# A two-layer H3 and MLP kernel: sums, powers and stage order of the normalisation between its first two units

## The chip, the cores and the metric

The kernel runs on one core of one Trainium2 chip. The metric is the device time in microseconds (us) of one execution. A core has five engines that run side by side, each in the order of its own instructions: TensorE (PE) multiplies matrices, VectorE (DVE), ScalarE (ACT) and GpSimd (POOL) work on elements, and SyncE (SP) starts transfers here. Semaphores order the engines among each other. On chip there are SBUF (128 partitions) and PSUM, where matrix products arrive.

## The reference

Two kinds of layer alternate, A, B, A, B, each added to its input. With S = 2048 tokens, D = 1024 channels and F = 3584 hidden columns, all in float32:

```python
def _A_ref(q, k, v, shift_k, ssm_k, ssm_D):     # q is the normalised x
    k_shift = short causal convolution of k with shift_k (4 taps)
    kv = k_shift * v
    y  = long causal convolution of kv with ssm_k (length S, by FFT) + kv * ssm_D
    return q * y

def _B_ref(x, w1, b1, w2, b2):                  # x is normalised
    h = relu(x @ w1 + b1) ** 2
    return h @ w2 + b2

x = A_q
x = x + _A_ref(_layernorm(x), ...);  x = x + _B_ref(_layernorm(x), ...)
x = x + _A_ref(_layernorm(x), ...);  x = x + _B_ref(_layernorm(x), ...)
```

The inputs k and v of the convolution do not depend on x, so the long convolution y is computed once and used by both A layers. The normalisation subtracts the row's mean and divides by the root of its variance plus 1e-5.

## The kernel before

Tokens are worked in four blocks of 512 (four tiles of 128 rows each, numbered 0 to 3 within the block). A unit is the B layer of one block at one depth, and ORDER lists them: layer 0 of block 0, layer 1 of block 0, layer 0 of block 1, layer 0 of block 2, and so on. Only the first change of units stays with its block (`direct`): unit 1 needs what unit 0 just finished. It therefore has to gate and normalise between two matrix products, while the other units are prepared beforehand.

A unit is a list of steps. A step of kind m1 multiplies one weight tile of w1 (128x512) with the transposed activations; one of kind m2 multiplies the squared activations with a tile of w2. Every product is done as three matmuls on numbers split into a high and a low part: the weight is loaded (`w_load`), its high part is cast on ScalarE (`w_hi`, L1112), the low part is a subtraction on VectorE or GpSimd (`w_lo`, L1120, engine by the table WLO); some split weights are stored and come back as pairs by one transfer (L1108). `w_advance` (L1130) issues all this some three steps ahead of the use, as far as six buffers go.

Around the first change of units the steps are halved, so that one half of the block (tiles 0 and 1) can be gated and normalised while TensorE works on the other: `add_halves` (L934) makes 28 m2 half steps, first both output halves for tiles 0 and 1, then for tiles 2 and 3; `add_ahead` (L950) makes 24 m1 half steps for six hidden tiles of unit 1, twelve for tiles 0 and 1, twelve for tiles 2 and 3. In half steps `tts` names two tiles, and so `len(tts) < NT`.

The work between is done by `chain` (L1737). When the accumulators of a half are complete, `evict1` adds the products to the residual (L1778) and takes statistics (L1779), and `lag.at(d, stage, cst, kk)` puts the stages 0 to 10 on a list, each d steps later; `lag.tick()` runs, once a step, what is due. The numbers d are the two rows of CHAIN. Stage 0 aggregates the statistics and starts a root on ScalarE (L732), stage 1 makes the scale by eight small VectorE operations (L738 to L754 and L1754). Stage 2 gates both tiles: ScalarE normalises a half row into PSUM (L1760), VectorE multiplies with y (L1767), adds to x (L1769) and takes statistics again (L1773). Stages 3 and 4 repeat the scale, 5 and 6 normalise the two tiles (L1808 on ScalarE, L1810 on VectorE, by NORM), 7 and 8 transpose them on TensorE (L1819), 9 and 10 split them into xh and xl (L1827, L1828). The tiles y come by `load_y` (L1731) into a ring of two buffers.

Beside the units, two generators prepare the long convolution of later blocks. The forward streams (`fwd_x`, `fwd_g`, one `fwd_tick` for both) transform kv and the filter; the product stream (`prod_stream`) multiplies spectra on GpSimd (L546) and sums them on VectorE (L550). At the end of each step the products get a budget: `pace` per step, a tenth of it in half steps; where the product stream has to wait for a transform (it yields None), the forward streams get a tick more. In half steps that is the only tick they get, since the line below (L2321) gives none. At the first half step of the change `closed[0] = True` (L2266) keeps the streams from taking the two PSUM banks "pt", and a loop runs the streams on until both are free.

The order inside a step is written in the main loop (L2163): in half steps of kind m1 (phase "x") the weights come first and the list after; in all others the list comes first.

Of the kernel before, what the change touches and what calls it, by code (L numbers as in the profile page):

```python
# [10 lines left out]
F32 = mybir.dt.float32  # L11
F32R = mybir.dt.float32r
BF16 = mybir.dt.bfloat16
AF = mybir.ActivationFunctionType
OP = mybir.AluOpType
# [4 lines left out]
S, D, F = 2048, 1024, 3584  # L20
P = 128
T = 512
NT = T // P
# [30 lines left out]
PLAIN = 1  # L54
PAD_C, PAD_P, PAD_M = 104, 104, 32
FILL = (16, 0, 8)
# [11 lines left out]
KEEP_M = 4  # L68
CHAIN = ((2, 3, 3, 7, 8, 8, 9, 13, 13, 14, 14), (2, 3, 3, 7, 8, 8, 9, 12, 12, 13, 13))
NORM = "VAVA"  # L70
WLO = {"b": "G", "x": "GGGV", "e": "G", "b1": "VVG", "c2": "VVG"}
# [180 lines left out]
def tile_h3_mlp(ctx: ExitStack, tc: tile.TileContext, q, kT, vT, shk, ssmT, ssmD, w1, b1, w2, b2,  # L252
# [474 lines left out]
    def rstd_a(mv):  # L727
        n = mv.shape[1]
        ve = pre.tile([P, n], F32, name="ve", bufs=3)
        V.tensor_scalar(ve, mv[:, :, 1], EPS, None, op0=OP.add)  # L730
        sd = pre.tile([P, n], F32, name="sd", bufs=3)
        A.activation(sd, mv[:, :, 1], AF.Sqrt, bias=epst)  # L732
        return ve, sd
# [1003 lines left out]
    def chain(accs, b, xh, xl, ready):  # L1737
        def bn(st, h):
            for n, tt in enumerate(st["tts"]):
                V.bn_stats(st["st"][:, n, h], accs[tt][:, h * 512:(h + 1) * 512])  # L1740

        def agg(st):
            mv = st["mv"] = pre.tile([P, 2, 2], F32, name="mv3", bufs=2)
            for n in range(2):
                V.bn_aggr(mv[:, n], st["st"][:, n])
            st["ve"], st["sd"] = rstd_a(mv)

        def newst(st):
            st["st"] = pre.tile([P, 2, 2, 6], F32, name="st3", bufs=2)

        def scales(st):
            r = st["r"] = rstd_b(st["ve"], st["sd"])
            st["nm"] = pre.tile([P, 2], F32, name="nm", bufs=3)
            V.scalar_tensor_tensor(st["nm"], st["mv"][:, :, 0], -1.0, r, op0=OP.mult, op1=OP.mult)  # L1754

        def scaled(st, n):
            out = []
            for h in range(2):
                z = ps1()
                A.activation(z, accs[st["tts"][n]][:, h * 512:(h + 1) * 512], AF.Identity,  # L1760
                             bias=st["nm"][:, n:n + 1], scale=st["r"][:, n:n + 1])
                out.append((h, z, accs[st["tts"][n]][:, h * 512:(h + 1) * 512], st["y"][n][:, h * 512:(h + 1) * 512]))
            return out

        def gate(ops):
            for h, z, x, y in ops:
                V.tensor_mul(z, z, y)  # L1767
            for h, z, x, y in ops:
                V.tensor_add(x, x, z)  # L1769

        def spread_of(st, n, ops):
            for h, z, x, y in ops:
                V.bn_stats(st["st"][:, n, h], x)  # L1773

        def evict1(st, os, dh):
            d = slice(dh * 512, (dh + 1) * 512)
            for n, tt in enumerate(st["tts"]):
                V.tensor_add(accs[tt][:, d], os[tt], accs[tt][:, d])  # L1778
                V.bn_stats(st["st"][:, n, dh], accs[tt][:, d])  # L1779

        def stage(st, k):
            tts = st["tts"]
            if k == 0:
                agg(st)
            elif k == 1:
                scales(st)
                newst(st)
            elif k == 2:
                ops = scaled(st, 0)
                gate(ops)  # L1790
                more = scaled(st, 1)
                spread_of(st, 0, ops)
                gate(more)
                spread_of(st, 1, more)
            elif k == 3:
                agg(st)
            elif k == 4:
                scales(st)
            elif k in (5, 6):
                n = k - 5  # L1800
                x, m, r = accs[tts[n]], st["mv"][:, n, 0:1], st["r"][:, n:n + 1]
                st["o", n] = []
                st["z", n] = [row() for _ in range(2)]
                for kh in range(2):
                    xn = st["z", n][kh]["t"]
                    xs = x[:, kh * 512:(kh + 1) * 512]
                    if NORM[2 * n + kh] == "A":
                        A.activation(xn, xs, AF.Identity, bias=st["nm"][:, n:n + 1], scale=r)  # L1808
                    else:
                        V.tensor_scalar(xn, xs, m, r, op0=OP.subtract, op1=OP.mult)  # L1810
                    st["o", n].append(xn)
            elif k in (7, 8):
# [8 lines left out]
                drop(*st["z", n])  # L1821
            else:
                n = k - 9
# [339 lines left out]
    for s, (k, u, c, a, i, tts, w) in enumerate(steps):  # L2163
# [30 lines left out]
        top = max(top, w)  # L2194
        if phase[0] == "x":
            w_advance(s, top)
            lag.tick()
        else:
            lag.tick()
            w_advance(s, top)  # L2200
# [105 lines left out]
        rate = pace.get(u, 100) * (PREP_PACE if busy else 1.0)  # L2306
        if len(tts) < NT:
            rate *= 0.1
        owed += rate
        todo = min(owed, BURST * rate)  # L2310
        while todo > 0:
# [63 lines left out]
```

## Time and profile before

| what | value |
|---|---|
| median of 3 runs | 2676.86 us (2676.43 to 2679.94) |
| the profiled execution, by the device clock | 2678.26 us |
| its span, first to last instruction | 2676.5 us |
| granted TensorE clock, mean | 0.995 |
| moved by transfers | 763.16 MB, mean 285 GB/s |
| splits of weights on VectorE (L1120, from raw weights) | 486 of 888 ns, 426.2 us |
| products on GpSimd (L546) | 288 of 1897 ns, 542.6 us |
| transposes of the chain (L1819) | 32, from 497.1 to 526.4 us |

The profile is of one execution, and its durations belong to that execution's 2678.26 us. "Busy" counts an engine from the start to the end of its instructions. Matmuls overlap, so TensorE's busy share says little of how fast it goes; the distance from one start to the next does. A row of waits names the engine and line that waited, the one that released it, the total, the number of waits and the longest. In rows of the timeline the first number is the start, the second the duration, and a bracket at the end gives idle time before it and what ended it. The granted clock is a share of full speed.

### The profile page before, as it was taken

How to read it: one execution, taken by the hardware profiler on the slowest of the kernel's cores; microseconds unless marked ns; L12 is line 12 of the kernel's file. 1: busy time of each engine (PE TensorE's matmuls, PEld its weight loads, DVE VectorE, ACT ScalarE, POOL GpSimd, SP SyncE). 2: the span in 40 equal slices, each digit the busy share in tenths (PEclk: the TensorE clock that was granted, in tenths of full speed). 3: DMA queues.
4: the chain of work that ended last, by engine and by line, in shares of the span. 5: the costliest groups of instructions: out<-in, count | busy, mean ns of one | idle time of the engine just before them, and what ended most of it. 6: DMA issues, size and time to landing. Idle time of an engine off the chain costs nothing.

```text
span 2676.5 us, 36110 instructions
## 1 busy us (share of the span) xinstructions
PE 2623.3 (98%) x12388; PEld 2198.9 (82%) x12388; DVE 1980.9 (74%) x2848; ACT 1133.8 (42%) x1931; POOL 1034.8 (39%) x683
## 2 busy tenths in 40 slices
PE   8899999899999999999999999999999999999999
PEld 7888787788888888888888888888788778888887
DVE  7878888789987777779777775456778767777553
ACT  5454344444444333343333422345444585454442
POOL 2436665255542645427554175000100217536111
PEclk9999999999999999999999999999999999999999
DMA  8799898689989998788987888689889798878653
GB/s 255 250 316 310 295 302 282 234 290 369 353 296 312 317 333 298 276 299 305 339 303 253 300 295 305 207 264 315 300 295 307 264 338 254 264 252 312 231 195 121
DMA packets 380265, 763.16 MB, mean 285 GB/s; under 512 B 44064, under 2 KB 159408, under 8 KB 377008
## 3 DMA queue, kind: packets, MB, share of 16 engines
q1 hardware_dynamic: 380080, 760.85, 83.3%
q8 instruction: 98, 1.61, 0.2%
q14 instruction: 87, 0.71, 0.1%
HBM read 583.49 MB, written 177.21 MB: 284 GB/s over the span
## 4 chain that ended last, share of the span: by engine, by line
PE 80%; DMA 6%; DVE 4%; ACT 2%; issue 1%; POOL 1%; SPq 0%; DVEq 0%; POOLq 0%; ACTq 0%
PE p L356 24%; PE p L357 24%; PE p L358 24%; PE pt L358 2%; PE pt L356 2%; PE pt L357 2%; DMA whl<-wd_m 2%; DMA wr<-w 1%; DMA wd_m<-whl 1%; DVE whl L1120 1%; DMA yt<-yd 0%; PE pt L412 0%; PE pt L441 0%; DMA cx<-xd 0%; PE pt L616 0%
## 5 line engine op out<-in xcount | busy, mean ns | idle before, releaser
L546 POOL TENSOR_TENSOR cp<-cx,cg 128x384 f32<-128x384 f32 (+5 forms) x288 | 542.6, 1897 | 569.2 <-DVE sm L550 374.6
L356 PE MATMUL p<-xh,whl 128*128 128x512 f32 (+1 forms) x1504 | 577.0, 384 | 6.3 <-DMA whl<-wd_m 5.7
L358 PE MATMUL p<-xh,whl 128*128 128x512 f32 (+1 forms) x1504 | 572.9, 381 | 3.3 <-DVE whl L1120 2.8
L357 PE MATMUL p<-xl,whl 128*128 128x512 f32 (+1 forms) x1504 | 572.8, 381 | 0.4 <-DVE xl L1515 0.4
L1112 ACT CAST whl<-wr 128x512 fp32r<-128x512 f32 x546 | 332.4, 619 | 466.4 <-PE p L358 275.1
L1120 DVE TENSOR_TENSOR whl<-wr,whl 128x512 fp32r<-128x512 f32 x486 | 426.2, 888 | 131.0 <-ACT whl L1112 130.3
L356 PE MATMUL p<-whl,rh 128*128 128x512 f32 x1204 | 477.1, 396 | 4.9 <-DMA whl<-wd_m 4.3
L357 PE MATMUL p<-whl,rh 128*128 128x512 f32 x1204 | 472.1, 392 | 2.5 <-POOL whl L1120 1.4
L358 PE MATMUL p<-whl,rl 128*128 128x512 f32 x1204 | 471.5, 392 | 0.0
L356 PEld LDWEIGHTS p<-xh,whl 128*128 128x128 f32 x1504 | 283.4, 188 | 61.1 <-DMA whl<-wd_m 2.5
L358 PEld LDWEIGHTS p<-xh,whl 128*128 128x128 f32 x1504 | 283.3, 188 | 58.3 <-DVE whl L1120 3.0
L357 PEld LDWEIGHTS p<-xl,whl 128*128 128x128 f32 x1504 | 283.5, 188 | 52.7 <-DVE xl L1515 0.6
L1607 DVE TENSOR_TENSOR rl<-wr,rh 128x512 fp32r<-128x512 f32 x140 | 142.2, 1016 | 177.9 <-ACT rh L1604 177.7
L356 PEld LDWEIGHTS p<-whl,rh 128*128 128x128 f32 x1204 | 227.9, 189 | 53.4 <-DVE fg L1716 3.3
L1120 POOL TENSOR_TENSOR whl<-wr,whl 128x512 fp32r<-128x512 f32 x60 | 87.3, 1458 | 475.9 <-ACT whl L1112 447.7
L357 PEld LDWEIGHTS p<-whl,rh 128*128 128x128 f32 x1204 | 227.9, 189 | 50.2 <-DVE whl L1120 2.7
L358 PEld LDWEIGHTS p<-whl,rl 128*128 128x128 f32 x1204 | 227.6, 189 | 48.0
L550 DVE TENSOR_REDUCE sm<-cp 128x128 f32<-128x384 f32 (+5 forms) x288 | 249.4, 874 | 10.2 <-POOL cp L546 10.2
L1599 ACT ACTIVATE wr<-p,b1t 128x512 f32<-128x512 f32 x138 | 95.3, 690 | 367.2 <-PE p L358 366.2
L1727 DVE TENSOR_TENSOR acc<-p,acc 128x512 f32<-128x512 f32 x152 | 100.0, 686 | 81.0 <-PE p L358 80.9
L696 POOL TENSOR_TENSOR sm<-sm 128x512 f32<-128x512 f32 x48 | 68.7, 1431 | 134.0 <-DVE sm L550 128.5
L356 PE MATMUL p<-whl,tq 128*128 128x512 f32 x276 | 107.4, 389 | 0.0
(393 smaller groups left out, 4280.5 us busy)
## 6 DMA issues: line engine op xcount, KB each, us to landing
whl<-wd_m SPq DMA_DIRECT2D x318, 512.0 KB, 5.5
wr<-w SPq DMA_DIRECT2D x442, 256.0 KB, 5.7
wd_m<-whl SPq DMA_DIRECT2D x70, 512.0 KB, 6.0
wr<-td SPq DMA_DIRECT2D x112, 256.0 KB, 5.0
cx<-xd SPq DMA_DIRECT2D x48, 512.0 KB, 5.9
cg<-gd SPq DMA_DIRECT2D x48, 512.0 KB, 6.8
tq<-hd SPq DMA_DIRECT2D x24, 1024.0 KB, 7.3
gd<-fg SPq DMA_DIRECT2D x72, 256.0 KB, 5.9
```

The lines of the kernel that those rows point to most:

```text
L356: PE.matmul(o, lh, rh, start=start, stop=False)
L357: PE.matmul(o, lh, rl, start=False, stop=False)
L358: PE.matmul(o, ll, rh, start=False, stop=stop)
L546: G.tensor_mul(pr.rearrange("p c i -> p i c"), xt[:, 0:j + 1], gt[:, j::-1])
L550: V.tensor_reduce(sm[:, ty, jj], st["pr"], axis=AX.X, op=OP.add)
L696: E.tensor_add(s[:, 1:3], s[:, 1:3], s[:, 0:1].to_broadcast([P, 2, s.shape[2]]))
L1112: A.copy(t[:, 0], raws[n]["t"])
L1120: ENG[e[n % len(e)]].tensor_sub(t[:, 1], raws[n]["t"], t[:, 0].bitcast(F32))
L1599: A.activation(r, st["o"], AF.Relu, bias=b1t[:, st["f"]:st["f"] + 1])
L1607: V.tensor_sub(st["lo"], st["r"]["t"], st["hi"].bitcast(F32))
L1727: V.tensor_add(accs[tt][:, d], o, accs[tt][:, d])
```

## The change

All of it concerns half steps, so the first change of units and, by the last two hunks, the eight half steps near the start.

- Sums: for the first tile of each half, the additions to the accumulator (`summed`) become one VectorE operation that also writes its row sum; ScalarE then squares the row with the mean as bias and sums it (`spread_a`). The second tile keeps VectorE's statistics.
- Powers: the scale is one addition, one power and one multiplication on GpSimd (`scale_of`), in place of the root on ScalarE and eight small operations on VectorE.
- Staged gating: stage 1 gates the first tile, stage 2 the second, stage 3 takes the second tile's statistics. CHAIN gets new due times, NORM another engine for one half row.
- Weights split ahead: in all half steps `w_advance` comes before `lag.tick()`.
- Products: none in half steps; the budget of a tenth is still added to what is owed.
- PAD_P pads a pool by 16 words a partition more.

```diff
-PAD_C, PAD_P, PAD_M = 104, 104, 32
+PAD_C, PAD_P, PAD_M = 104, 120, 32
-CHAIN = ((2, 3, 3, 7, 8, 8, 9, 13, 13, 14, 14), (2, 3, 3, 7, 8, 8, 9, 12, 12, 13, 13))
-NORM = "VAVA"
+CHAIN = ((2, 3, 5, 8, 9, 8, 10, 13, 13, 14, 14), (2, 3, 5, 7, 7, 6, 9, 11, 12, 12, 13))
+NORM = "AAVA"
...
+        def summed(st, n, d, z):
+            x = accs[st["tts"][n]][:, d * 512:(d + 1) * 512]
+            V.scalar_tensor_tensor(x, z, 1.0, x, op0=OP.mult, op1=OP.add, accum_out=st["c"][:, 4 + d:5 + d])
+
+        def spread_a(st):
+            c = st["c"]
+            V.tensor_scalar(c[:, 0:1], c[:, 4:5], c[:, 5:6], -1.0 / (root * D), op0=OP.add, op1=OP.mult)
+            junk = ml.tile([P, D], BF16, name="yt", bufs=2)
+            A.activation(junk, accs[st["tts"][0]], AF.Square, scale=1.0 / root, bias=c[:, 0:1], accum_out=c[:, 1:2])
+            scale_of(st, 0, c[:, 1:2], c[:, 0:1], root)
...
+        def scale_of(st, n, var, m, k):
+            o = st["rn"][:, n]
+            G.tensor_add(var, var, epst)
+            G.tensor_tensor(o[:, 0:1], var, eph[:, 1:2], op=OP.pow)
+            G.tensor_scalar(o[:, 1:2], m, o[:, 0:1], k, op0=OP.mult, op1=OP.mult)
...
-        def gate(ops):
-            for h, z, x, y in ops:
+        def gate(st, n, ops):
+            x = accs[st["tts"][n]]
+            for z, y in ops:
                 V.tensor_mul(z, z, y)
-            for h, z, x, y in ops:
-                V.tensor_add(x, x, z)
+            for h, (z, y) in enumerate(ops):
+                if n:
+                    V.tensor_add(x[:, h * 512:(h + 1) * 512], x[:, h * 512:(h + 1) * 512], z)
+                else:
+                    summed(st, 0, h, z)
...
         def evict1(st, os, dh):
             d = slice(dh * 512, (dh + 1) * 512)
-            for n, tt in enumerate(st["tts"]):
-                V.tensor_add(accs[tt][:, d], os[tt], accs[tt][:, d])
-                V.bn_stats(st["st"][:, n, dh], accs[tt][:, d])
+            t0, t1 = st["tts"]
+            summed(st, 0, dh, os[t0])
+            if dh == (t0 > 0) ^ 1:
+                spread_a(st)
+            V.tensor_add(accs[t1][:, d], os[t1], accs[t1][:, d])
+            V.bn_stats(st["st"][:, 0, dh], accs[t1][:, d])
...
         def stage(st, k):
             tts = st["tts"]
             if k == 0:
-                agg(st)
+                spread_v(st)
+                scale_v(st)
             elif k == 1:
-                scales(st)
+                st["g"] = scaled(st, 0)
+                st["old"] = dict(st)
                 newst(st)
+                gate(st, 0, st["g"])
+                spread_a(st)
             elif k == 2:
-                ops = scaled(st, 0)
-                gate(ops)
-                more = scaled(st, 1)
-                spread_of(st, 0, ops)
-                gate(more)
-                spread_of(st, 1, more)
+                gate(st, 1, scaled(st["old"], 1))
             elif k == 3:
-                agg(st)
+                for h in range(2):
+                    V.bn_stats(st["st"][:, 0, h], accs[tts[1]][:, h * 512:(h + 1) * 512])
+                spread_v(st)
             elif k == 4:
-                scales(st)
+                scale_v(st)
             elif k in (5, 6):
...
+                normal(st, k - 5)
...
-        if phase[0] == "x":
+        if len(tts) < NT:
             w_advance(s, top)
             lag.tick()
         else:
...
-        if len(tts) < NT:
-            rate *= 0.1
-        owed += rate
-        todo = min(owed, BURST * rate)
+        owed += rate * (0.1 if len(tts) < NT else 1.0)
+        todo = 0.0 if len(tts) < NT else min(owed, BURST * rate)
         while todo > 0:
```

More of the change, by code (lines that the diff above doesn't have):

```diff
@@ L1737, in chain, with spread_v, scale_v @@
     def chain(accs, b, xh, xl, ready):
[L1738 to L1754 removed]
+        root = math.sqrt(D)
+        def summed(st, n, d, z):
[7 more added lines that the diff above has]
+            scale_of(st, 0, c[:, 1:2], c[:, 0:1], root)
+        def spread_v(st):
+            st["mv"] = pre.tile([P, 1, 2], F32, name="mv3", bufs=2)[:, 0]
+            V.bn_aggr(st["mv"], st["st"][:, 0])
+        def scale_v(st):
+            scale_of(st, 1, st["mv"][:, 1:2], st["mv"][:, 0:1], -1.0)
+        def scale_of(st, n, var, m, k):
[3 more added lines that the diff above has]
+            G.tensor_scalar(o[:, 1:2], m, o[:, 0:1], k, op0=OP.mult, op1=OP.mult)
+        def newst(st):
+            st["st"] = pre.tile([P, 1, 2, 6], F32, name="st3", bufs=2)
+            st["c"] = pre.tile([P, 6], F32, name="nr", bufs=4)
+            st["rn"] = pre.tile([P, 2, 2], F32, name="mv2", bufs=4)
         def scaled(st, n):
@@ L1821, in stage @@
                 drop(*st["z", n])
-            else:
+            elif k > 8:
                 n = k - 9
```

32 lines of the change are left out of this document (14 added, 18 removed).

## The prediction

> **What bounds the kernel now.** I read the page first (engine shares), then the stages (busy time and granted clock by window), then TensorE's waits in the stretch that the change touches, then the timelines of single engines there.
>
> ```profile
> span 2676.5 us, 36110 instructions
> PE 2623.3 (98%) x12388; PEld 2198.9 (82%) x12388; DVE 1980.9 (74%) x2848; ACT 1133.8 (42%) x1931; POOL 1034.8 (39%) x683
> ```
>
> TensorE is the bound: it idles 53.2 us in all, and only matmuls that start late can be won or lost. So the question is where those idle stretches lie, and the rows by window answer it (us, then busy time and count of PE, PEld, DVE, ACT, POOL, then granted clock, DMA share, GB/s).
>
> ```profile
> 250.00:300.00 50.00, 43.04 (x197) 35.68 (x195) 43.30 (x63) 19.36 (x36) 28.95 (x24) 0.96 0.90 305
> 300.00:350.00 50.00, 49.80 (x225) 41.88 (x226) 36.88 (x59) 18.91 (x35) 23.32 (x20) 0.94 0.81 256
> 400.00:450.00 50.00, 47.76 (x224) 39.86 (x223) 45.21 (x66) 21.58 (x40) 30.96 (x24) 0.97 0.84 275
> 456.80:503.17 46.37, 42.34 (x186) 32.81 (x184) 34.86 (x64) 20.99 (x34) 11.51 (x10) 1.00 0.84 298
> 503.17:547.01 43.84, 39.55 (x314) 38.73 (x312) 31.19 (x50) 21.83 (x36) 18.72 (x10) 0.96 0.57 191
> 550.00:600.00 50.00, 50.00 (x250) 42.50 (x249) 39.80 (x64) 16.54 (x30) 21.16 (x14) 1.00 0.95 312
> 513.50:521.00 7.50, 4.71 (x27) 4.57 (x26) 5.67 (x17) 1.81 (x3) 1.31 (x2) 0.77 0.46 162
> ```
>
> The change of units is the fourth and fifth row: 456.80 to 503.17 are the 28 half steps that end the first unit, 503.17 to 547.01 the 24 half steps that begin the second. TensorE idles 4.0 + 4.3 us in them. The clock of 0.96 in the fifth row is another loss that idle time doesn't show. The waits of TensorE in the two stretches (us in total, times, longest):
>
> ```profile
> PE p L357 <- POOL whl L1120: 1.4, 2, 0.9
> PE p L357 <- DVE whl L1120: 1.0, 2, 0.8
> PE p L1819 <- DVE xl L1828: 1.0, 1, 1.0
> PE p L356 <- DMA whl<-wd_m: 0.5, 1, 0.5
> ...
> PE p L358 <- DVE whl L1120: 2.8, 1, 2.8
> PE p L1819 <- DVE xl L1828: 1.0, 1, 1.0
> ```
>
> Above the dots is the first stretch, below them the second. The 2.8 us are the largest, and cost more than they show:
>
> ```profile
> 513.36 0.28 PE L357 MATMUL p<-xl,whl 128*128 128x256 f32 x1
> 516.43 0.39 PE L358 MATMUL p<-xh,whl 128*128 128x256 f32 x1 [2.79 <-DVE whl L1120]
> ...
> 519.27 0.41 PE L356 MATMUL pt<-xh,whl 128*128 128x256 f32 x1
> 519.48 0.41 PE L357 MATMUL pt<-xl,whl 128*128 128x256 f32 x1
> ...
> 522.10 0.28 PE L356 MATMUL pt<-xh,whl 128*128 128x256 f32 x1
> 522.22 0.28 PE L357 MATMUL pt<-xl,whl 128*128 128x256 f32 x1
> ```
>
> From start to start a matmul of 256 columns takes 0.12 us at 522, 0.21 at 519. The gap took 516.43 - 513.36 - 0.12 = 2.95 us, and the granted clock of 0.77 over 7.5 us (1.7 us lost) is the slow stretch behind it. Together 4.6 us, the largest loss in the change of units.
>
> **The change part by part.**
>
> *Staged gating.* Why was that weight late? VectorE's timeline:
>
> ```profile
> 508.43 1.40 DVE L1767 TENSOR_TENSOR p<-p,px 128x512 f32<-128x512 f32 x2 [0.85 <-ACT p L1760]
> ...
> 514.51 1.28 DVE L1773 BATCH_NORM_STATS2 st<-acc 128x6 f32<-128x512 f32 x2
> 515.71 0.67 DVE L1120 TENSOR_TENSOR whl<-wr,whl 128x512 fp32r<-128x512 f32 x1
> ```
>
> One stage issues twelve operations in a row (two products, two sums, two statistics, for each of two tiles), 508.43 to 515.7, and the split of the weight (L1120) stands behind all of them. The change makes two stages of it, two ticks apart. The first holds only two products and two sums with the row sum taken along, four operations. Their price comes from the rows below: with 0.75 for a sum, 2 x 0.70 + 2 x 0.75 = 2.9 us. Ahead of them ScalarE squares the first tile and GpSimd makes the scale:
>
> ```profile
> L1760 ACT ACTIVATE p<-acc,nm,rs 128x512 f32<-128x512 f32 x8 | 5.9, 773 | 5.4 <-DVE acc L1769 2.8 <-DVE nm L1754 2.6
> L486 DVE SCALAR_TENSOR_TENSOR pt<-fk,sgn,pt 128x512 f32<-128x512 f32 x24 | 17.9, 748 | 0.0
> L723 ACT ACTIVATE jk<-px,co 128x1024 bf16<-128x1024 f32 x8 | 9.2, 1150 | 0.3
> L723 ACT ACTIVATION_READ_ACCUMULATOR jk<-px,co 128x1 f32 x8 | 1.5, 187 | 0.0
> L724 POOL TENSOR_TENSOR co<-co,eph 128x1 f32<-128x1 f32 x8 | 1.8, 230 | 52.6 <-ACT jk L723 52.6
> L725 POOL TENSOR_TENSOR co<-co,eph 128x1 f32<-128x1 f32 x8 | 4.8, 606 | 0.6
> L1892 POOL TENSOR_SCALAR co<-co 128x1 f32<-128x1 f32 x4 | 1.1, 267 | 0.4
> ```
>
> From the end of the last product before the second stretch (about 502.7): row sum 0.75 and a small operation 0.2 on VectorE, square 1.34 on ScalarE, three small ones 1.1 on GpSimd, which makes 3.5 us with hand-overs; ScalarE normalises a half in 0.77 (L1760) and the four gating operations follow it to about 7.4 us, so 510.1. The split follows until 510.8, before 513.4. So the 2.95 us and the 1.7 us of slow clock go: **-4.6**. The second tile's gate comes a stage later, done at about 13.7 us; its normalising ends near 17 by the same durations, and its transposes stand at the twelfth step (502.7 + 0.5 + 11 x 12 x 0.12 = 519.0, which is 16.3) behind 1.0 us of the first tile's. So nothing there is late by more than about half a microsecond. Moving the first tile's transposes a tick ahead (12 to 11 in the second row of CHAIN) hides half of the 1.0 us at L1819 behind a step: **-0.5**. The other L1819 wait stays, its two places remain 13 and 13.
>
> *Sums and powers.* Statistics of one tile of two leave VectorE, and its eight small operations per scale become three on GpSimd. An unknown is the sum with its accumulator, which VectorE never runs here. Bounds: 0.75 (the row above) to 0.75 + 0.19 (ScalarE's read of its accumulator); below 0.75 nothing speaks for it. I take 0.75, its own engine's row; eight of them at the other end cost 1.5 us of VectorE, half on the two chains, inside their slack. The Trainium skill ("VectorE: DVE Perf Modes", Two Vector instructions with no wait between them) says that an operation which also writes out its accumulator is two instructions, so it speaks for the upper end; no run here shows it on VectorE, on ScalarE the second row of L723 does. By it I would save at most 0.8 us less, 2671.3 in place of the time below.
>
> *Weights ahead.* In half steps the splitting is now issued before the chain's stages. Queued behind the waiting chain before were casts on ScalarE and splits on GpSimd (1.4 us) and VectorE (1.0). They are late because of what stands ahead. But the new square on ScalarE waits for VectorE's gate, and the casts of the following steps queue behind it, as do GpSimd's splits behind the scale, with TensorE behind them. And the next thing that is late is a transfer:
>
> ```profile
> 477.56 0.68 DVE L1778 TENSOR_TENSOR acc<-p,acc 128x512 f32<-128x512 f32 x1
> ...
> 487.77 1.28 DVE L1767 TENSOR_TENSOR p<-p,px 128x512 f32<-128x512 f32 x2
> 489.49 0.38 SPq L1108 DMA_DIRECT2D whl<-wd_m  x1
> whl<-wd_m SPq DMA_DIRECT2D x318, 512.0 KB, 5.5
> ```
>
> The queue of SP holds the load of the second y tile until the gate has read the first ones (487.77 + 1.28 = 489.05, 11.5 us behind the accumulators' last sums), and the weight pair behind it starts at 489.49, lands some 5.5 us later, at 495, and TensorE waits 0.5 for it. That release comes no earlier after the change: the second gate is now a stage later, and the sum of the same durations as above (3.5 for the scale, 3.9 for the first gate, 1.3 for its square, 1.5 + 1.4 for the second) puts it 11 to 12 us behind the accumulators. So TensorE can't reach that weight much before 495, whatever it saves ahead of it: of the 1.4 I keep 0.6, of the 1.0, which lies in the first unit's last sums and moves all that follows, 0.7. **-1.3**, bounds -3 and +2 (a new wait of 2 us).
>
> *Products paused.* Only two of them run between 484 and 532, the first one is
>
> ```profile
> 499.13 1.29 POOL L546 TENSOR_TENSOR cp<-cx,cg 128x512 f32<-128x512 f32 x1
> ```
>
> so the pause frees 2.3 us of an engine that waits anyway: nothing, and the few products left over run in the second unit, where TensorE has no idle time (550 to 600: 50.00 of 50.00 busy). PAD_P (16 words more) only makes up for smaller statistics tiles: nothing.
>
> *What the pause moves besides.* With no product asked for, the forward transforms get no tick in the eight half steps near the start. Before, they did:
>
> ```profile
> 127.09 0.43 SPq L376 DMA_DIRECT2D fx<-kT  x1
> PE pt L441 <- DVE fx L388: 7.2, 2, 5.0
> PE pt L616 <- ACT whl L1112: 2.2, 1, 2.2
> SPq L514 <- DVE fg L505: 8.2, 1, 8.2
> ```
>
> So both streams start eight ticks later, some three full steps (about 9 us), and keep that lag through the first unit. There TensorE waits 7.2 us for L388 in 260 to 360 and 2.2 us at 442, where the queue of SP stood 8.2 us for L505. With 2.0 + 3.0 + 1.5 us of clock (0.96, 0.94, 0.97 of 50 us) that is 15.9 us, all chance meetings of the streams with evictions and weights. The lag deals these cards anew. Its mean is nothing; the bounds are -10 (two of three meetings gone) and +12 (two more like the worst, 5.0 + 1.5).
>
> **Sum.** -4.6 - 0.5 - 1.3 = -6.4 us. The profiled execution took 2678.26 us (1.8 around its span), 1.4 more than the median of 2676.86: 2676.86 - 6.4 = **2670.5**.
>
> **The rivals.**
>
> *Cover eaten* (2676.9). ScalarE's square (1.34 us) stands behind the gate (2.9 us), so casts wait over 4 us in each half; two new waits of some 3 us take what the staged gate gave. For it: casts already wait behind ScalarE's normalising in the first stretch. Against: weights in the second stretch are issued a step or more ahead.
>
> *Streams meet the change* (2684). Three steps late, the last group of the first transform of that block still holds both PSUM banks when the half steps begin, and the program must run it out there (the loop behind the closing of the banks). Its stores then hold the queue of SP, as L514 did for 8.2 us, while half steps use up weights twice as fast. Price: two waits like those at 442 and 300 with their clock, 4 + 8 = 12, with the 6.4 won: +6, 2683 to 2684. It decides once the first unit and this place lose more than 11.8 us over the 15.9. Against: the wait at 442 is the same event, and may just move.
>
> *Streams miss each other* (2662). Two of the three waits in the first unit vanish, another -8.
>
> *It isn't what it says.* The pause pauses next to nothing, as shown; that is in the sum.
>
> *The clock.* A gap of 2.24 us at 442 and one of 2.79 at 513 were each followed by slow matmuls. The Trainium skill ("TensorE: Matmul & The Clock Gate", HAM oscillation) wants no gaps above about 3.4 us; by that the 1.7 us wouldn't hang on this gap and 2672.2 would come out. The trace disagrees (2.79 us, then 0.77), so it gets no chance of its own.
>
> **How the numbers follow.** A measurement of this kernel can tell about 0.2% (5.4 us) from no change. Forecast 0.45 (0.35 of it beyond 0.2%, 0.10 within), cover eaten 0.25, streams meet 0.18, streams miss 0.12. Faster 0.35 + 0.12 = 0.47, same 0.35, slower 0.18. The range for 8 in 10 reaches from a little below the miss to the meeting: 2660 to 2684. The forecast's own range is 2666 to 2675.
>
> **What would show it.** Right: no wait of TensorE on L1120 above 1 us in the second stretch, clock 1.00 there, both stretches together 84 us in place of 90.2; VectorE's rows show gates of four operations with a weight's split between them; the load of the y tiles still ahead of the pair that lands last. Wrong: TensorE waiting for casts behind the square; L441 or L616 waits in the first unit summing to something other than 9.4 us; stores of L514 within the first half steps.

## The result and the profile after

The changed kernel took 2701.07 us (median of 4 runs, 2696.97 to 2707.90), the kernel before beside it 2678.15 us: a ratio of 1.0091, 95% interval 1.0077 to 1.0104. It is slower by 0.9%, and the forecast of 2670.5 us with its range up to 2684 was wrong. The profiled execution is the slowest of the four, 2707.9 us, with this on its page (the span, then busy time, share and instructions by engine):

```profile
span 2706.1 us, 36100 instructions
PE 2629.5 (97%) x12388; PEld 2200.0 (81%) x12388; DVE 1989.5 (74%) x2818; ACT 1137.5 (42%) x1937; POOL 1043.2 (39%) x707
```

TensorE now idles 76.6 us in place of 53.2. Where, the rows by window tell (us, busy time and count of the five engines, granted clock, DMA share, GB/s). The first fence is the kernel after: the 28 half steps that end the first unit, the 24 that begin the second, the rest of unit 1 to the first step of unit 2, and units 2 and 3 as far as step 450. The second fence is the kernel before in the last two of these stretches; its first two stand in the prediction.

```profile
456.09:508.80 52.71, 45.51 (x188) 35.12 (x187) 29.49 (x56) 21.89 (x36) 10.28 (x17) 0.94 0.72 257
508.80:547.89 39.09, 36.92 (x306) 36.33 (x304) 26.31 (x33) 24.12 (x39) 22.08 (x21) 1.00 0.61 203
547.89:866.69 318.80, 309.57 (x1462) 258.56 (x1461) 266.07 (x378) 129.09 (x230) 151.67 (x97) 0.98 0.90 309
866.69:1449.26 582.57, 573.50 (x2698) 479.52 (x2696) 465.56 (x591) 203.57 (x364) 286.61 (x154) 1.00 0.88 305
```

```profile
547.01:848.96 301.95, 301.33 (x1442) 253.29 (x1441) 261.39 (x373) 127.58 (x229) 138.30 (x85) 1.00 0.94 326
848.96:1419.65 570.69, 570.18 (x2697) 478.61 (x2696) 443.85 (x587) 203.45 (x362) 287.34 (x154) 1.00 0.88 309
```

The first half step stands at 456.1 us, before at 456.8: the first unit lost nothing in these two profiles. The first stretch is 6.3 us longer (52.71 against 46.37), the second 4.8 shorter (39.09 against 43.84). The loss lies where nothing was changed: 16.8 us in unit 1 and 11.9 in units 2 and 3, in both of which TensorE had almost no gap before. Its waits there (line waiting, line waited for, us in total, times, longest), first in unit 1, below the dots in units 2 and 3:

```profile
PE p L358 <- DVE whl L1120: 4.2, 1, 4.2
PE pt L357 <- DVE fx L402: 2.7, 1, 2.7
PE p L356 <- DMA whl<-wd_m: 1.9, 1, 1.9
...
PE p L356 <- DMA whl<-wd_m: 5.2, 5, 2.0
PE p L357 <- DVE whl L1120: 2.4, 1, 2.4
PE p L356 <- DVE acc L1727: 1.4, 1, 1.4
```

What stood ahead of the weight that came 4.2 us late is in VectorE's timeline (start, duration, line, operation):

```profile
628.16 4.98 DVE L386 SCALAR_TENSOR_TENSOR fx<-fx,shkt 128x512 f32<-128x512 f32 x3
...
635.60 0.94 DVE L550 TENSOR_REDUCE sm<-cp 128x128 f32<-128x768 f32 x1
636.47 2.08 DVE L582 TENSOR_TENSOR yl<-sm,yh 128x256 fp32r<-128x256 f32 x2
638.47 0.68 DVE L1120 TENSOR_TENSOR whl<-wr,whl 128x512 fp32r<-128x512 f32 x1
```

A transform of the forward streams (L386), the sum of a product (L550) and the split of an inverse (L582) are all issued in the steps just ahead of that split. So the streams and the products stand in other places than before. Which of them does it, and what put them there?

### The profile page after: what moved, and what is told of

Its sections match the earlier page's. It is cut to its first block, busy times and chain, and to the rows that moved or that the text cites. A ratio compares the mean times of both kernels' runs of the same rounds, so it can differ in the third digit from the quotient of the medians.

```text
span 2706.1 us, 36100 instructions
## 1 busy us (share of the span) xinstructions
PE 2629.5 (97%) x12388; PEld 2200.0 (81%) x12388; DVE 1989.5 (74%) x2818; ACT 1137.5 (42%) x1937; POOL 1043.2 (39%) x707
## 4 chain that ended last, share of the span: by engine, by line
PE 74%; DMA 10%; DVE 5%; issue 2%; POOL 2%; ACT 1%; SPq 1%; DVEq 0%; POOLq 0%; ACTq 0%
PE p L356 22%; PE p L357 22%; PE p L358 22%; DMA whl<-wd_m 3%; DMA wr<-w 2%; PE pt L358 2%; PE pt L357 2%; PE pt L356 2%; DMA cg<-gd 2%; DVE whl L1120 1%; DMA cx<-xd 1%; POOL acc L1869 1%; DMA wd_m<-whl 1%; DVE fx L386 0%; PE pt L616 0%
## 5 line engine op out<-in xcount | busy, mean ns | idle before, releaser
L356 PE MATMUL p<-xh,whl 128*128 128x512 f32 (+1 forms) x1504 | 579.6, 385 | 11.6 <-DMA whl<-wd_m 10.4
L1120 DVE TENSOR_TENSOR whl<-wr,whl 128x512 fp32r<-128x512 f32 x486 | 442.9, 922 | 135.0 <-ACT whl L1112 127.3
L550 DVE TENSOR_REDUCE sm<-cp 128x128 f32<-128x384 f32 (+5 forms) x288 | 249.3, 874 | 26.8 <-POOL cp L546 26.8
L1607 DVE TENSOR_TENSOR rl<-wr,rh 128x512 fp32r<-128x512 f32 x140 | 136.4, 975 | 168.1 <-ACT rh L1604 167.9
L1120 POOL TENSOR_TENSOR whl<-wr,whl 128x512 fp32r<-128x512 f32 x60 | 87.4, 1459 | 428.5 <-ACT whl L1112 406.9
```

Source lines behind the costliest of these rows:

```text
L356: PE.matmul(o, lh, rh, start=start, stop=False)
L550: V.tensor_reduce(sm[:, ty, jj], st["pr"], axis=AX.X, op=OP.add)
L1120: ENG[e[n % len(e)]].tensor_sub(t[:, 1], raws[n]["t"], t[:, 0].bitcast(F32))
L1607: V.tensor_sub(st["lo"], st["r"]["t"], st["hi"].bitcast(F32))
```

## The experiments

**Theories.** Lag: the eight ticks that the forward streams lose at the start shift them for good, and that makes the new waits. Backlog, later called arrears: products not made in the change of units are made up close together in unit 1. Chain: the staged gating and the weights ahead shift the stretches and all behind them. All ratios are to the kernel before on the same chip, with a 95% interval. Unless another kernel is named, an experiment edits the changed kernel. The table has each kernel's profiled durations by window, in the four stretches of above (us). Each is of one execution, and the first stretch varies most: the twelve experiments that have both the new chain and the weights ahead measure 45.8 to 50.4 us there.

| kernel | ratio | first stretch | second stretch | rest of unit 1 | units 2 and 3 to step 450 |
|---|---|---|---|---|---|
| before | 1 | 46.4 | 43.8 | 302.0 | 570.7 |
| after | 1.0091 | 52.7 | 39.1 | 318.8 | 582.6 |
| e1 start as before | 1.0026 | 50.2 | 39.2 | 311.7 | 571.2 |
| e2 pace as before | 0.9981 | 48.4 | 39.2 | 300.9 | 570.8 |
| e3 pause alone | 1.0100 | 47.7 | 42.0 | 318.8 | 580.3 |
| e4 weights first alone | 1.0007 | 50.0 | 43.7 | 303.3 | 570.6 |
| e5 arrears spread | 1.0038 | 48.7 | 39.1 | 304.4 | 580.2 |
| e6 the same, start as before | 1.0062 | 47.1 | 39.2 | 308.6 | 584.6 |
| e7 lag taken back | 1.0072 | 48.7 | 39.1 | 317.6 | 570.6 |
| e8 lag alone | 1.0034 | 48.2 | 39.2 | 302.8 | 579.6 |
| e9 chain alone | 0.9993 | 47.0 | 39.2 | 302.3 | 571.2 |
| e10 streams ahead | 0.9989 | 48.4 | 39.2 | 303.0 | 570.5 |
| e11 pause, both mended | 1.0017 | 45.8 | 39.2 | 309.2 | 570.9 |
| e12 all paused, both mended | 1.0085 | 50.3 | 39.1 | 309.4 | 580.2 |
| e13 one tick late | 0.9981 | 50.0 | 39.2 | 301.9 | 571.2 |
| e14 two ticks late | 1.0040 | 50.4 | 39.2 | 302.0 | 581.8 |
| e15 all paused, in time | 1.0021 | 50.0 | 39.1 | 308.4 | 570.5 |

**e1: pause in the change of units alone.** Eight half steps at the start ask for products as before, so the streams get their ticks there.

```diff
-        owed += rate * (0.1 if len(tts) < NT else 1.0)
-        todo = 0.0 if len(tts) < NT else min(owed, BURST * rate)
+        if len(tts) < NT and u == 0 and k == "m1":
+            rate *= 0.1
+        paused = len(tts) < NT and (u or k == "m2")
+        owed += rate * (0.1 if paused else 1.0)
+        todo = 0.0 if paused else min(owed, BURST * rate)
```

> The changed kernel, with products asked for as before in the eight half steps near the start, and paused only in the change of units. Lag theory (the forward streams lose eight ticks at the start, and this lag alone makes the new waits in the units behind the change): waits of TensorE between 555 and 1400 us fall back to under 5 us, time 2680 +- 6. Backlog theory (products not made in the change of units come later and take GpSimd and the queue of SP): no gain, 2695 or more. Chain theory (the staged gating and the weights ahead shift the two stretches and all behind them): no gain, 2695 or more.

Measured 1.0026 (1.0015 to 1.0037). Units 2 and 3 are whole again; unit 1 still loses 9.8 us over the kernel before. Each of lag and backlog had a part of it right, neither the whole. What the 9.8 us are, the program's order tells at e6.

**e2: pacing as before.** Only the chain and the weights ahead are left.

```diff
-        owed += rate * (0.1 if len(tts) < NT else 1.0)
-        todo = 0.0 if len(tts) < NT else min(owed, BURST * rate)
+        if len(tts) < NT:
+            rate *= 0.1
+        owed += rate
+        todo = min(owed, BURST * rate)
```

> The changed kernel with the whole pacing of products as before; what is left of the change is the chain and the weights ahead. Lag theory and backlog theory: 2680 +- 6 (by the forecast's own sum 2671). Chain theory: 2695 or more.

Measured 0.9981 (0.9971 to 0.9991), faster than both kernels, and than the 2680 +- 6 us that lag and backlog expected (it took 2671.5, the forecast's own sum). The chain theory falls: with the chain in place, units 1 to 3 lose nothing. Its stretches by window:

```profile
454.00:502.42 48.42, 42.05 (x185) 32.89 (x184) 27.97 (x52) 21.80 (x35) 13.01 (x20) 1.00 0.84 296
502.42:541.62 39.20, 37.80 (x314) 37.22 (x312) 28.18 (x35) 24.13 (x39) 26.20 (x25) 1.00 0.63 213
```

**e3: pause alone**, the same two lines of the diff put into the kernel before.

> The kernel before with the pause of products alone (start and change of units). Lag theory and backlog theory: slower by 15 to 30, 2692 to 2707. Chain theory: 2678 +- 5.

Measured 1.0100 (1.0081 to 1.0119). The pause alone makes all of the slowdown, in the same stretches as the change: 318.8 and 580.3 us.

**e4: weights first alone**, in the kernel before:

```diff
-        if phase[0] == "x":
+        if len(tts) < NT:
```

> The kernel before with the weights issued ahead of the chain's stages in all half steps, nothing else. Lag theory and backlog theory: 2678 +- 5, the forecast's sum says 1.3 faster. Chain theory, if the weights' place is its part: the first stretch of half steps longer by some 6 us and the time 2685 or more.

Measured 1.0007 (0.9998 to 1.0016). The time is that of the kernel before, as lag and backlog expected, but in its profile the first stretch is 3.6 us longer. TensorE's waits there:

```profile
PE p L1819 <- DVE xl L1828: 2.0, 1, 2.0
PE p L356 <- ACT whl L1112: 1.9, 2, 1.5
PE p L356 <- DMA whl<-wd_m: 1.7, 1, 1.7
```

Before, the first was 1.0 and the second did not stand among the waits. ScalarE's timeline in the changed kernel, where the first of them is longest (3.6 us), shows how they come about. In that kernel the lines of the chain have other numbers: L1838, L1846 and L1847 are L1819, L1827 and L1828 of the kernel before.

```profile
498.45 0.62 ACT L1112 CAST whl<-wr 128x512 fp32r<-128x512 f32 x1 [3.15 <-DMA wr<-w]
500.41 0.62 ACT L1112 CAST whl<-wr 128x512 fp32r<-128x512 f32 x1 [1.34 <-DMA wr<-w]
500.94 1.06 ACT L1846 CAST xh<-p 128x512 fp32r<-128x512 f32 x2
```

Two casts of weights wait for their transfer, and the cast of the transposed activations (L1846), whose transposes ended at 498.7 us, is queued behind the second of them since weights are now issued first.

**e5: arrears made up slowly.** The program's own order, that is the order in which it issues its instructions, tells how far behind the products are. With the pacing as before, 94 products are issued by the end of the change of units; in the changed kernel it is 84, four missing from the change itself and six from the lag of the streams, which feed them. It then owes 4.10 budget units. This kernel spreads the debt:

```diff
+        if u == 1 and s == start_step[1] + 24:
+            back = owed + 0.38
+            owed -= back
+        if u == 1 and 24 <= s - start_step[1] < 96:
+            owed += back / 72
...
+        if 164 <= s < 169:
+            fowed += 1
```

> The changed kernel, with the products that it owes at the end of the change of units (4.10 budget units, ten products fewer than without the pause) made up evenly over the next 72 steps, where the changed kernel makes one product a step until they are made up, some 34 steps. The forward streams get five ticks in their place, so that their lag stays what it is in the changed kernel (within one tick). Arrears theory (products made close together take VectorE and GpSimd from the weights between 560 and 720 us, which costs the changed kernel some 18 us over the kernel with the pacing as before): 2683 +- 5. Lag theory (the forward streams, three ticks late for good, cost all of it): stays 2697 or more.

Measured 1.0038 (1.0025 to 1.0051), as the arrears theory had it. The rest of unit 1 falls from 318.8 to 304.4 us, while units 2 and 3 keep their loss (580.2).

But by the program's order the ten products are not what costs. The changed kernel makes them at two a step, steps 158 to 163, and these six steps take 19.2 us in it as in e2. At step 166 it stands where e2 stands, in products and in debt (2.25 units). Only its streams are late: the transforms that the products wait for end three to five steps later. So at step 170 it owes 4.02 units where e2 owes 2.61, and it makes one product in every step from 173 to 189, e2 from 170 to 181. Between steps 164 and 194 it loses 14.8 us to e2, of 17.9 in all of unit 1. It is this longer run that e5 spreads; as far as these runs tell, it takes late streams and catching up together.

**e6: the same for the pause in the change alone** (e1), with one tick given at step 165.

> The kernel with the pause in the change of units alone, its smaller arrears (1.41 units, four products) made up evenly over 72 steps, one tick given to the streams for it. Arrears theory: the 12 us that this kernel lost over the one with the pacing as before come back, 2672 +- 4. Lag theory (one tick late): stays at 2680 or more.

Measured 1.0062 (1.0045 to 1.0079), a miss on both counts: unit 1 gains only 3.2 us over e1, and units 2 and 3 lose 13.4. The edit had put the streams one tick further back than e1 had them. Why one tick should cost 13 us in units 2 and 3 stayed open until e14. For unit 1 the program's order tells why spreading gains so little: in e1 the four products are made in steps 158 to 160, and behind it products stand at e2's steps; only the streams are one tick late. Of the 10.9 us that e1 loses to e2 in unit 1, 7.4 lie between steps 194 and 206. There a matmul of the streams waits 4.8 us, until 688 us, for VectorE's L424, which stands behind the split of an inverse (L582) in e1 and ahead of it in e2.

**e7 and e8: lag given back and lag alone.** Three ticks more in the changed kernel, three fewer in e2, at step 210:

```diff
+        if s == 210:
+            fowed += 3
```

> The changed kernel, with three extra ticks of the forward streams at step 210 (about 700 us), where the arrears have been made up; from there on products and streams stand at the same steps as in the kernel with the pacing as before. Lag theory for what lies behind 880 us: the waits at 889, 930, 1183, 1256 and 1328 us vanish, 2701 - 9 = 2692. Rival (they come from elsewhere): 2701 +- 4.

> The changed kernel with the pacing as before and no arrears, but three ticks of the forward streams withheld at step 210 (about 680 us), so that they run as late behind it as in the changed kernel. Lag theory for what lies behind 880 us: 2671.5 + 9 = 2680, with waits of TensorE near 860 to 1310 us that this kernel has not without the lag. Rival: 2671.5 +- 4.

Measured 1.0072 (1.0057 to 1.0087) and 1.0034 (1.0021 to 1.0047). Units 2 and 3 by window, first e7, then e8, and below them TensorE's waits there in e8:

```profile
865.07:1435.66 570.59, 570.06 (x2697) 478.80 (x2696) 451.83 (x587) 203.62 (x362) 290.01 (x154) 1.00 0.88 309
```

```profile
847.38:1426.99 579.61, 571.75 (x2698) 478.28 (x2696) 463.64 (x591) 203.54 (x364) 287.19 (x154) 1.00 0.88 307
```

```profile
PE p L356 <- DMA whl<-wd_m: 4.1, 5, 1.4
PE p L357 <- DVE whl L1120: 2.4, 1, 2.4
PE p L356 <- DVE acc L1727: 1.4, 1, 1.4
```

In e7, with the lag taken back, the three rows are gone (0.5 us is left in all); with the lag alone they are there, two of them to the tenth as in the changed kernel. The loss in units 2 and 3 is the lag.

**e9: chain alone**, e2 with the order of weights and stages as before.

```diff
-        if len(tts) < NT:
+        if phase[0] == "x":
```

> The kernel before with the sums, the powers and the staged gating alone; pacing of the products and place of the weights as before. In the runs so far the second stretch of half steps was 4.7 us shorter wherever the new chain stood, and the first stretch 3.6 us longer where the weights alone were issued ahead. If these two are apart from each other: second stretch 39 us, first stretch 46.4 or less, total 1.5 to 3 us below the kernel with chain and weights (0.9981), so a ratio of 0.9970 +- 0.001. Rival (the weights ahead belong to the new chain, whose square on ScalarE would else hold up their casts): first stretch 48 or more, ratio 0.998 or above.

Measured 0.9993 (0.9984 to 1.0001): not the 0.9970 hoped for. The first stretch is 47.0 us, 1.4 below e2, but a new wait stands in it:

```profile
PE p L357 <- POOL whl L1120: 2.8, 1, 2.8
```

With the stages first, GpSimd's split of a weight is queued behind the powers that the chain now puts on GpSimd, which there wait 3.9 us for ScalarE's square. So each order has a wait of its own with this chain, and between e2 and e9, whose intervals overlap, the runs don't decide.

**e10: streams three ticks ahead**, `fowed += 3` at step 210 in e2.

> The changed kernel with the pacing as before, and the forward streams given three extra ticks at step 210, so that behind it they run three ticks early where another run had them three ticks late. If late streams are bad as such: ratio 0.998, no new waits. If any place but the one of the kernel before meets other work (each lag so far had waits of its own): new waits of 3 to 12 us behind 700 us, ratio 0.999 to 1.003.

Measured 0.9989 (0.9980 to 0.9998), no new waits behind step 210 (1.6 us of them stand ahead of it): the idea that any other place of the streams would cost something falls. In issue order the lead shrinks to nothing by the second x transform (a transform of kv, by `fwd_x`) of block 3, so unit 3 did not test it.

**e11: e6 with four ticks given**, steps 165 to 168, in place of one.

> The kernel with the pause in the change of units alone, its arrears made up over 72 steps, and four ticks given back to the streams just behind the change, so that from step 169 on they stand where they stand with the pacing as before (the run before this one with spread arrears had them two ticks late). If arrears and lag are all that the pause costs: the 3.9 us wait near 617 us and the waits near 911, 1167 and 1241 us go, ratio 0.998 to 0.9995. If products missing in the change cost by themselves: 1.0025 or more.

Measured 1.0017 (1.0007 to 1.0026), between the two expectations. Units 2 and 3 are whole. Unit 1 keeps 309.2 us, and most of what it loses is one wait, from 580 to 585 us, among the four ticks given one after the other:

```profile
PE pt L356 <- ACT wr L622: 4.9, 1, 4.9
```

**e12: e5 with five more ticks**, every second step from 206 to 214.

> The changed kernel with its whole pause, start included; its arrears (ten products) spread over 72 steps, as in the run with a ratio of 1.0038, and five more ticks given to the forward streams between steps 206 and 214, one every second step, so that from there on they stand where the pacing as before has them. Arrears and lag together: unit 1 loses 2 to 4 us as in that run, units 2 and 3 nothing, so 2675 +- 4 (ratio 0.9985 to 1.0015), against 1.0091 for the change. If the pause costs in a third way: 1.004 or more.

Measured 1.0085 (1.0067 to 1.0102), a plain miss. Counting ticks was not enough: a stream that waits for a PSUM bank spends its tick without getting on. By the steps in which transforms end, the streams of e12 are still a step or two late in units 2 and 3, and the window shows the loss (580.2). That is not all of it: e5 has the same loss there and measured 1.0038. In unit 1 the two, which are the same program up to step 206, agree within 0.2 us as far as that, and e12 loses 5 us more behind it, among its extra ticks. And e12's first half step stands at 463.1 us where the changed kernel, with the same program so far, has 456.1 and e5 454.0; what moves the first unit by 9 us is not known.

**e13, e14, e15: where the cost of the lag begins.** By those steps, the kernels with a whole unit 2 and 3 share one thing: the sixth x transform of block 2 ends at or before step 238. Behind it come the last steps of unit 1, 239 to 257, in which the streams get no ticks. In the others it ends at steps 258 to 262. e13 and e14 are e2 with one and two ticks withheld at step 210; e15 is e12 with its extra ticks earlier, at steps 196, 200, 204, 208, 212 and 216.

> The changed kernel with the pacing as before, and one tick of the forward streams withheld at step 210. The sixth x transform of block 2 still ends in its step, before the 18 steps without ticks. Threshold theory: units 2 and 3 lose nothing (below 1 us), ratio 0.998 to 0.9995. Proportional theory (three ticks cost 9 us): 3 us, ratio 0.9992 to 1.0005, with some of the waits near 910, 1163 and 1236 us.

> The same with two ticks withheld: the sixth x transform of block 2 now ends twenty steps later, behind the change to unit 2. Threshold theory: the whole loss of 9 to 14 us, with the waits near 910, 1163 and 1236 us, ratio 1.0015 to 1.004. Proportional theory: 6 us, ratio 1.000 to 1.0015.

> The changed kernel with its whole pause and its arrears spread as before, and six ticks given to the streams one by one between steps 196 and 216, so that the sixth x transform of block 2 ends in time. Threshold theory: units 2 and 3 lose below 1 us; unit 1 loses 2 to 8 us as in the other runs with spread arrears; with a first unit as in the change (within 4 us) 2672 to 2684, ratio 0.9985 to 1.003. If a lag at any time costs: the waits of units 2 and 3 return, 1.005 or more.

Measured 0.9981 (0.9972 to 0.9991), 1.0040 (1.0025 to 1.0055) and 1.0021 (1.0011 to 1.0032), all three as the threshold has it. Units 2 and 3 by window, e13, e14 and e15:

```profile
843.87:1415.03 571.16, 570.25 (x2697) 478.65 (x2696) 447.83 (x587) 203.52 (x362) 288.94 (x154) 1.00 0.88 309
```

```profile
843.68:1425.43 581.75, 573.61 (x2698) 480.81 (x2696) 466.04 (x589) 203.42 (x364) 288.94 (x154) 0.99 0.87 304
```

```profile
851.51:1421.97 570.46, 569.93 (x2697) 478.74 (x2696) 449.65 (x587) 203.57 (x362) 289.70 (x154) 1.00 0.88 309
```

The second late tick costs 10.6 us there, the first 0.4 (over e2's 570.8). The largest wait of e14 is for a weight's split, 4.1 us, and its VectorE and GpSimd timelines show it from inside; below them is VectorE of e13 at the same step:

```profile
1227.86 2.77 DVE L386 SCALAR_TENSOR_TENSOR fx<-fx,shkt 128x512 f32<-128x512 f32 x1
1230.56 2.62 DVE L1607 TENSOR_TENSOR rl<-wr,rh 128x512 fp32r<-128x512 f32 x1
...
1234.09 1.03 DVE L388 TENSOR_TENSOR fx<-fx 128x512 f32<-128x512 f32 x1
1235.05 2.85 DVE L1120 TENSOR_TENSOR whl<-wr,whl 128x512 fp32r<-128x512 f32 x1
```

```profile
1227.24 2.85 POOL L1869 TENSOR_TENSOR acc<-acc,px 128x1024 f32<-128x1024 f32 x1
1230.04 2.59 POOL L546 TENSOR_TENSOR cp<-cx,cg 128x896 f32<-128x896 f32 x1
...
1234.54 2.82 POOL L546 TENSOR_TENSOR cp<-cx,cg 128x1024 f32<-128x1024 f32 x1
```

```profile
1220.59 2.90 DVE L388 TENSOR_TENSOR fx<-fx 128x512 f32<-128x512 f32 x1
1223.40 2.89 DVE L1607 TENSOR_TENSOR rl<-wr,rh 128x512 fp32r<-128x512 f32 x1
1226.22 1.07 DVE L550 TENSOR_REDUCE sm<-cp 128x128 f32<-128x896 f32 x1
1227.21 1.63 DVE L1120 TENSOR_TENSOR whl<-wr,whl 128x512 fp32r<-128x512 f32 x1
```

In e13 the short convolution that opens a transform (L386, then L388) is through before L1607 of that step; in e14 L388 comes behind it and ahead of the split, and the split, beside a product on GpSimd of 2.82 us, takes 2.85 in place of 1.63. That is one meeting of three; why all three turn on this one point of the program is not shown.

## Why the prediction was wrong

**Staged gating (-4.6): right, the clock's share of it partly by luck.** The second stretch measures 39.1 to 39.2 us in all fourteen kernels with the new chain against 43.8 before: 4.7 us. In e3, with the old chain, the same gap (there 2.40 us) was not followed by slow matmuls: the clock was 1.00 and the stretch 42.0 us. Against that profile the new chain is worth 2.8. VectorE has the gate of four operations, with the weight's split right behind it:

```profile
513.24 1.40 DVE L1781 TENSOR_TENSOR p<-p,px 128x512 f32<-128x512 f32 x2 [2.58 <-ACT p L1773]
514.55 0.68 DVE L1742 SCALAR_TENSOR_TENSOR acc<-p,acc 128x512 f32<-128x512 f32 x1
515.16 0.08 DVE L1742 DVE_READ_ACCUMULATOR acc<-p,acc 128x1 f32 x1
...
516.07 0.69 DVE L1120 TENSOR_TENSOR whl<-wr,whl 128x512 fp32r<-128x512 f32 x1
```

The clock there is 1.00. The waits that the changed kernel has left in this stretch:

```profile
PE p L358 <- POOL whl L1120: 1.4, 1, 1.4
PE p L1838 <- DVE xl L1847: 0.8, 1, 0.8
```

VectorE's split is no longer waited for; one on GpSimd is, for 1.4 us, which the forecast's sign ("no wait of TensorE on L1120 above 1 us") had excluded.

**Transposes a tick ahead (-0.5): not gained.** The last row is about what it was, 0.8 us here and 0.9 in e2 against 1.0 before.

**Sums and powers: right in size.** A sum takes 0.68 us and the read of its accumulator 0.08, together about the lower bound of 0.75. The Trainium skill ("VectorE: DVE Perf Modes", Two Vector instructions with no wait between them) states that an operation which also writes out its accumulator is two instructions; the trace agrees, the second is the row of 0.08 us.

**Weights ahead (-1.3, bounds -3 and +2): not gained.** Alone it makes the first stretch 3.6 us longer (e4), with the new chain some 2 (47.0 in e9, a mean of 48.8 in the twelve experiments that have both), each by few profiles that differ by more than that. The prediction looked for casts behind the square and for the late transfer, but not the other way round: chain casts behind casts of weights that wait for a transfer. The changed kernel shows the worst case, 52.7 us; those twelve measured 45.8 to 50.4, so its 6.3 us are partly chance; some 3 of them are slow clock (0.94 over the stretch). Here "cover eaten" was the nearest rival, by another mechanism.

**The sum without the pause: inside the interval, partly by luck.** -6.4 us is a ratio of 0.9976, inside the interval of e2 (0.9971 to 0.9991). But in e2's profile the two stretches take 87.6 us together, where the forecast had 84 in place of 90.2: -4.6 came, -0.5 and -1.3 did not. The rest of its lead lies elsewhere, more than half of it in the first unit (2.8 us), whose end varies by more than that from kernel to kernel.

**Products paused: miscounted, but cheap by itself.** "so the pause frees 2.3 us of an engine that waits anyway: nothing, and the few products left over run in the second unit, where TensorE has no idle time". Ten products were left over, not two, since the lag at the start had already put six in arrears. Made up at two a step, they cost nothing that shows (19.2 us for steps 158 to 163, in e2 as well).

**What the pause moves besides: the step that failed.** The streams "keep that lag through the first unit", says the prediction, and "Its mean is nothing". In the first unit that fits: it ended 0.7 us earlier than before, and its ends with the pause at the start, at 452.9 to 463.1 us in six profiles, overlap those of the eleven without it, at 450.9 to 457.2. But the lag does not end with the unit, and what comes behind was put at nothing without a reason.

In unit 1 the late transforms keep the products waiting, and the longer run of one product a step behind them costs 15 to 18 us (318.8 against 300.9 to 303.3 without the pause). No idle time on TensorE did not mean room on the engines that feed it. With the debt spread over 72 steps, 1 to 9 us are left (e5, e12, e15 against those). No run has these late streams without the ten products owed, so the two are told apart by the program's order alone. The 6 to 8 us that unit 1 loses in e6, e11, e12 and e15 are not traced one by one.

The streams run on until 1400 us and more, and where they are late enough for one transform to miss the end of unit 1, units 2 and 3 lose 9 to 14 us, in seven kernels of seven (after, e3, e5, e6, e8, e12, e14); in all others they stay within 0.7 us of the kernel before. The prediction took a schedule's shift for a new deal of the same cards with mean nothing. In stretches without a gap there was nothing to win by it, only to lose, and that was readable beforehand: 50.00 of 50.00 busy from 550 to 600.

**The other rivals.** The streams did meet the change (three stores of L514 run at 458 us, two us into the half steps), but the wait like that at 442 us before (2.2 us at L616) now ends at 455, just ahead of the half steps, and none came within them. "Streams miss each other" did not occur: the waits of L441 and L616 between 130 and 456 us sum to 10.7 us, before to 10.0.

So the 29 us between the change and e2 (1.10% of 2676.86) are, taken in this order, 12 from the pause in the change of units (e1 against e2) and 17 from the eight half steps at the start (the change against e1). A version that keeps all of the change but the pause, e2, beats both kernels, by 0.19% and by 1.1%.

## What to carry to other kernels

When background work is paused, follow it to its end: count what it owes afterwards, at which pace that is made up, what waits for the work that has become late, and which later deadline a late stream will miss. Where the bottleneck engine has no gap, a shifted schedule can only cost, so the risk there is one-sided and the range has to reach that way. A tick of pacing is not progress; measure the lag by the step in which a piece of work ends.

## What the runs showed of the hardware

VectorE's price for one operation depends on GpSimd. In the changed kernel L388 (128x512, both inputs in SBUF) takes 0.68 us at 633.73 us, where no GpSimd operation runs beside it:

```profile
633.73 0.68 DVE L388 TENSOR_TENSOR fx<-fx 128x512 f32<-128x512 f32 x1
```

In e13 it took 2.90 beside GpSimd's additions (three of L1869 in 8.49 us, so 2.83 each): a factor of four, and nearly the duration of the GpSimd operation. That is the far end. Of the 24 such operations of the changed kernel, the 11 without a GpSimd operation beside them have a median of 0.68 us, the other 13 one of 1.1. The Trainium skill ("SBUF — State Buffer", Who interferes with whom) states that a VectorE instruction with two SBUF inputs contends with a GpSimd instruction that reads SBUF; these rows agree. In e14 it is enough to account for the 4 us by which the weight is late: L386, L1607 and the split take 2.77, 2.62 and 2.85 us beside GpSimd, 8.2 together, where their medians without it in the changed kernel are 0.75, 0.69 and 0.68.

Slow matmuls behind a gap are a matter of chance here until the gap is long. In the traces of all seventeen kernels, between 90 and 2600 us, a fall of the granted clock to half, for 3.4 or 6.8 us, began during the gap or within 4.2 us of its end at 38 of 67 TensorE gaps of 2 to 3 us, at all 28 above 3.5 us, and at 6 of 193 between 0.95 and 1.8 us. So a gap of 2.8 us does not carry its slow stretch with certainty: before it did (0.77 over 7.5 us), and in e3 one of 2.40 us at the same place did not.
